# Four heads side by side on the array, and the other matmuls woven between them, in a gated mix of attention and FFN with its gradients

## The chip, the cores and the metric

The kernel runs on one core of one Trainium2 chip. The metric is device time in microseconds (us) of one execution. Unless a run says otherwise, times are medians of several executions.

## The reference, cut to what matters

The function computes a sigmoid gate `g`, a sliding-window attention `a` (32 heads of 16 features, window 256, sequence 2048, model width 512), a gated FFN `b` (width 1376), and the output `g * a + (1 - g) * b`. The kernel must return this output and the gradients of seven inputs.

```python
def _A_ref(x, wqkv, wo):
    H = 32; Dh = D // H; W = 256                    # Dh = 16
    q, k, v = ...                                   # (cut) x @ wqkv, split by head
    scores = jnp.einsum("bhqd,bhkd->bhqk", q, k) * (Dh ** -0.5)
    mask = (idx[:, None] - idx[None, :] >= 0) & (idx[:, None] - idx[None, :] < W)
    p = _softmax(jnp.where(mask[None, None], scores, -1e9), axis=-1)
    o = jnp.einsum("bhqk,bhkd->bhqd", p, v)
    return o.transpose(...).reshape(B, S, D) @ wo
def _B_ref(x, W_gate, W_up, W_down):
    gate = x @ W_gate; up = x @ W_up                # (written as einsum)
    return ((gate * (gate > 0)) * up) @ W_down
g = _sigmoid((x * gate_w).sum(-1, keepdims=True))
out = g * a + (1 - g) * b
def reference(..., grad_out):                       # (cut)
    _out, _vjp = jax.vjp(_f, A_x, A_wqkv, A_wo, B_W_gate, B_W_up, B_W_down, gate_w)
    return (_out, *_vjp(grad_out))
```

The backward pass of attention needs, for each head, the scores S, their exponentials P, the products dP = dO V^T, P * dP, and four weighted sums of these with K, V, Q and dO. The kernels compute them twice, once with queries and once with keys on the partitions.

## The kernel before: the parts that matter here

The program runs in stages: the FFN and its weight gradients, then attention in four groups of eight heads, then the weight gradients of the projections and the outputs. In attention, K and V are stored once for each head with zeros in the rows of the other seven heads (`KTz`, `VTz`), so that a matmul over all 128 rows gives the scores of one head. This is the pass by query blocks (the pass by key blocks is alike):

```python
for j in range(NT):                                  # 16 query blocks of 128
    kbs = list(range(max(0, j - 2), j + 1))
    ...
    for h8 in range(HG):                             # 8 heads
        ST = psA.tile([P, 3, P], F32, tag="ST")
        nc.tensor.matmul(ST[:, nb - 1, :], lhsT=ident[:], rhs=mbd[:, 0, :], ...)   # the mask
        for i, kb in enumerate(kbs):
            nc.tensor.matmul(ST[:, i, :], lhsT=KTz[:, h8, kb * P:(kb + 1) * P],
                             rhs=QT[:, j * P:(j + 1) * P], start=False, stop=True, ...)
        nc.scalar.activation(PuT[:, :nb, :], ST[:, :nb, :], ACT.Exp, scale=scale)
        ...                                          # affine_select on POOL where nb == 3
        for i, kb in enumerate(kbs):
            nc.tensor.matmul(dPT[:, i, :], lhsT=VTz[:, h8, kb * P:(kb + 1) * P],
                             rhs=dOT[:, j * P:(j + 1) * P], start=True, stop=True)
        nc.vector.tensor_tensor(out=PdPT[:, :nb, :], in0=PuT[:, :nb, :], in1=dPT[:, :nb, :], op=ALU.mult)
        for i, kb in enumerate(kbs):                 # 33 columns
            nc.tensor.matmul(Bacc[:, h8, :], lhsT=PuT[:, i, :], rhs=KV1[:, kb, h8, :], ...)
        for i, kb in enumerate(kbs):                 # 17 columns
            nc.tensor.matmul(Aacc[:, h8, :], lhsT=PdPT[:, i, :], rhs=KV1[:, kb, h8, 0:17], ...)
```

The softmax here doesn't subtract the row's maximum and nothing guards it: scores larger than these inputs give would overflow.

Of the kernel before, what the change touches and what calls it, by code (L numbers as in the profile page):

```python
# [9 lines left out]
ALU = mybir.AluOpType  # L10
# [3 lines left out]
I32 = mybir.dt.int32  # L14
# [4 lines left out]
WINDOW = 256  # L19


@with_exitstack
def kernel(
# [30 lines left out]
    assert Dh == 16 and D % P == 0 and S % P == 0 and WINDOW == 2 * P  # L54
    NT = S // P
    DC = D // P
    HG = P // Dh
    FC = (F + P - 1) // P
    TGW = min(512, S)
    NTG = S // TGW  # L60
    TPG = TGW // P
    scale = float(Dh) ** -0.5
    C3 = 3 * DC
# [3 lines left out]

    rr = {"i": 0}

    def evac(out, in_, eng=None):  # L70
        if eng is None:
            eng = ("act", "dve")[rr["i"] % 2]
            rr["i"] += 1
        if eng == "act":
            nc.scalar.copy(out, in_)  # L75
        elif eng == "dve":
            nc.vector.tensor_copy(out, in_)
        else:
            nc.gpsimd.tensor_copy(out, in_)

    def bc(ap2, n):
# [3 lines left out]
    hT_d = dram.tile([F, S], BF, name="hT_d")  # L85
    dgT_d = dram.tile([F, S], BF, name="dgT_d")
    duT_d = dram.tile([F, S], BF, name="duT_d")
    dqkv_d = dram.tile([S, 3 * D], BF, name="dqkv_d")
    O_d = dram.tile([S, D], BF, name="O_d")

    cpool = ctx.enter_context(tc.tile_pool(name="const", bufs=1))
    ident = cpool.tile([P, P], BF, name="ident")
    make_identity(nc, ident[:])
    NEG = -30000.0
    mbd = cpool.tile([P, 2, P], BF, name="mbd")
    nc.gpsimd.memset(mbd[:], 0.0)
    nc.gpsimd.affine_select(out=mbd[:, 0, :], in_=mbd[:, 0, :], compare_op=ALU.is_ge, fill=NEG,
                            base=0, pattern=[[1, P]], channel_multiplier=-1)
    nc.gpsimd.affine_select(out=mbd[:, 1, :], in_=mbd[:, 1, :], compare_op=ALU.is_ge, fill=NEG,
                            base=0, pattern=[[-1, P]], channel_multiplier=1)  # L100
    zeros_sb = cpool.tile([P, 512], F32, name="zeros_sb")
    nc.vector.memset(zeros_sb[:], 0.0)
    gw_b = cpool.tile([P, D], BF, name="gw_b")
    nc.sync.dma_start(gw_b[:], gate_w.partition_broadcast(P))
    g_all = cpool.tile([P, NT], F32, name="g_all")
    omg_all = cpool.tile([P, NT], F32, name="omg_all")
    z_all = cpool.tile([P, NT], F32, name="z_all")

    xT_pool = tc.tile_pool(name="xT", bufs=1, side="right")
    xT_pool_obj = xT_pool.__enter__()  # L110
    x_T = xT_pool_obj.tile([P, DC, S], BF, name="x_T")
    da_T = xT_pool_obj.tile([P, DC, S], BF, name="da_T")

    def transpose_rows_to_T(dst_T, src_r, psum_pool):
        for c in range(DC):
            for t0 in range(0, NT, 8):
                n = min(8, NT - t0)
                pt = psum_pool.tile([P, 8, P], BF, tag="tr")
                for k in range(n):
                    nc.tensor.transpose(pt[:, k, :], src_r[:, t0 + k, c * P:(c + 1) * P], ident[:])  # L120
                evac(dst_T[:, c, t0 * P:(t0 + n) * P].rearrange("p (k s) -> p k s", k=n), pt[:, :n, :])

    with ExitStack() as p12:
        actp = p12.enter_context(tc.tile_pool(name="acts", bufs=1))
        x_r = actp.tile([P, NT, D], BF, name="x_r")
        db_r = actp.tile([P, NT, D], BF, name="db_r")
        db_T = actp.tile([P, DC, S], BF, name="db_T")
        nc.sync.dma_start_transpose(out=x_T[:], in_=x_d)
        nc.sync.dma_start(x_r[:], x_d.rearrange("(t p) d -> p t d", p=P))

        ps2 = p12.enter_context(tc.tile_pool(name="p2ps", bufs=1, space=PSUM))

        def tr_rows(dst_T, src_r):
            for c in range(DC):
                for t0 in range(0, NT, 8):
                    n = min(8, NT - t0)
                    pt = ps2.tile([P, 8, P], BF, tag="tr", bufs=2)
                    for k in range(n):
                        nc.tensor.transpose(pt[:, k, :], src_r[:, t0 + k, c * P:(c + 1) * P], ident[:])
                    evac(dst_T[:, c, t0 * P:(t0 + n) * P].rearrange("p (k s) -> p k s", k=n), pt[:, :n, :])  # L140

        wp = p12.enter_context(tc.tile_pool(name="ffw", bufs=1))
        Wg_sb = wp.tile([P, DC, F], BF, name="Wg_sb")
        Wu_sb = wp.tile([P, DC, F], BF, name="Wu_sb")
        WdT_sb = wp.tile([P, DC, F], BF, name="WdT_sb")
        nc.scalar.dma_start(Wg_sb[:], B_W_gate.rearrange("(c p) f -> p c f", p=P))
        nc.scalar.dma_start(Wu_sb[:], B_W_up.rearrange("(c p) f -> p c f", p=P))
        fp = p12.enter_context(tc.tile_pool(name="ffn", bufs=2))
        with ExitStack() as p1:
            tmpp = p1.enter_context(tc.tile_pool(name="p1tmp", bufs=1))  # L150
            for c in range(DC):
                nc.scalar.dma_start_transpose(out=WdT_sb[:, c, :], in_=B_W_down[:, c * P:(c + 1) * P])
            gw_col = tmpp.tile([P, DC], BF, name="gw_col")
            nc.sync.dma_start(gw_col[:], gate_w.rearrange("(c p) -> p c", p=P))
            zps = ps2.tile([P, NT], F32, tag="wg", bufs=2)
            for t in range(NT):
                for c in range(DC):
                    nc.tensor.matmul(zps[:, t:t + 1], lhsT=x_T[:, c, t * P:(t + 1) * P], rhs=gw_col[:, c:c + 1],
                                     start=(c == 0), stop=(c == DC - 1))
            nc.scalar.activation(g_all[:], zps[:], ACT.Sigmoid)  # L160
            nc.vector.tensor_scalar(omg_all[:], g_all[:], -1.0, 1.0, op0=ALU.mult, op1=ALU.add)
            for t in range(NT):
                go_t = tmpp.tile([P, D], BF, tag="go_t", bufs=4)
                nc.gpsimd.dma_start(go_t[:], go_d[t * P:(t + 1) * P, :])
                nc.scalar.mul(db_r[:, t, :], go_t[:], omg_all[:, t:t + 1])
                da_t = tmpp.tile([P, D], BF, tag="da_t", bufs=3)
                nc.vector.tensor_scalar(da_t[:], go_t[:], g_all[:, t:t + 1], None, op0=ALU.mult)
                for src, dst in ((db_r[:, t, :], db_T), (da_t[:], da_T)):
                    pt = ps2.tile([P, 8, P], BF, tag="tr", bufs=2)
                    for c in range(DC):  # L170
                        nc.tensor.transpose(pt[:, c, :], src[:, c * P:(c + 1) * P], ident[:])
                    evac(dst[:, :, t * P:(t + 1) * P], pt[:, :DC, :])

        with ExitStack() as p2:
            for fc in range(FC):
                fs = fsz(fc)
                f0 = fc * P
                rg = fp.tile([P, S], BF, tag="rg")
                upm = fp.tile([P, S], BF, tag="upm")
                hT = fp.tile([P, S], BF, tag="hT")  # L180
                dgT = fp.tile([P, S], BF, tag="dgT", bufs=1)
                duT = fp.tile([P, S], BF, tag="duT", bufs=1)
                for tg in range(NTG):
                    ts_ = slice(tg * TGW, (tg + 1) * TGW)
                    gps = ps2.tile([P, TGW], F32, tag="mm", bufs=4)
                    ups = ps2.tile([P, TGW], F32, tag="mm", bufs=4)
                    for c in range(DC):
                        nc.tensor.matmul(gps[:fs, :], lhsT=Wg_sb[:, c, f0:f0 + fs], rhs=x_T[:, c, ts_],  # L188
                                         start=(c == 0), stop=(c == DC - 1))
                    for c in range(DC):  # L190
                        nc.tensor.matmul(ups[:fs, :], lhsT=Wu_sb[:, c, f0:f0 + fs], rhs=x_T[:, c, ts_],  # L191
                                         start=(c == 0), stop=(c == DC - 1))
                    nc.scalar.activation(rg[:fs, ts_], gps[:fs, :], ACT.Relu)
                    nc.vector.scalar_tensor_tensor(out=upm[:fs, ts_], in0=rg[:fs, ts_], scalar=0.0,  # L194
                                                   in1=ups[:fs, :], op0=ALU.is_gt, op1=ALU.mult)
                    nc.gpsimd.tensor_tensor(out=hT[:fs, ts_], in0=rg[:fs, ts_], in1=upm[:fs, ts_], op=ALU.mult)  # L196
                nc.sync.dma_start(hT_d[f0:f0 + fs, :], hT[:fs, :])
                for tg in range(NTG):
                    ts_ = slice(tg * TGW, (tg + 1) * TGW)
                    dhps = ps2.tile([P, TGW], F32, tag="mm", bufs=4)  # L200
# [222 lines left out]
    with ExitStack() as p56:  # L423
# [33 lines left out]
        with ExitStack() as p5:  # L457
# [12 lines left out]
            def load_round(ri, with_x=False):  # L470
                lo, hi = span(rounds[ri])
                if hi == lo:
                    return None, 0
# [199 lines left out]
```

## Time and profile before

| kernel before | |
|---|---|
| time | 1464.81 us, median of 3 runs (1462.81 to 1466.41) |
| feed-forward, from 0 us | about 330 us |
| attention, 330 to 1144 us | about 814 us |
| weight gradients and outputs, 1144 to 1465 us | about 321 us |
| matmuls | 16120 |

Some parts of the profile's page of the kernel before follow. Part 1 gives busy time and share of the span for each engine (PE is the matmul engine, PEld its weight loads, which overlap it). Part 2 cuts the span into 40 equal slices, each digit a busy share in tenths; PEclk is the granted clock of PE in tenths of full speed. Part 4 is the chain of work that ended last. Part 5 lists groups of instructions: line, engine, operation, out<-in, shapes, count, busy us, mean ns, then the idle time before them and what ended it.

```profile
...
PE 1226.8 (84%) x16120; PEld 882.4 (60%) x16120; DVE 805.4 (55%) x1801; ACT 733.6 (50%) x1706; POOL 677.2 (46%) x1894
...
PE   1899999996886998877988879988889558799996
...
PEclk9999999998998998998989989989979779899998
DMA  9212122123001011001030010110010692455530
...
PE 57%; ACT 12%; DVE 8%; POOL 7%; DMA 7%; issue 6%; ACTq 2%; SPq 1%; DVEq 0%; POOLq 0%
...
L331 DVE TENSOR_TENSOR PdPT<-PuT,dPT 128x384 bf16<-128x384 bf16 (+2 forms) x512 | 248.6, 521 | 66.1 <-POOL PuT L324 31.1
L322 ACT ACTIVATE PuT<-ST 128x384 bf16<-128x384 f32 (+2 forms) x512 | 230.6, 479 | 89.2 <-PE ST L318 68.2
...
L318 PE MATMUL ST<-QT,KTz 128*128 128x128 bf16 x1440 | 194.4, 224 | 1.9 <-DMA KTz<-KTn 1.8
...
L334 PE MATMUL BAp<-KV,PuT 128*128 128x33 bf16 x1440 | 117.0, 180 | 34.7 <-POOL PuT L324 31.6
...
```

The reader is to see two things. PE is busy in almost every slice, so PE is what bounds this kernel; the chain agrees with 57%. And PE's work is in small pieces: 1440 matmuls of 128 columns (224 ns each) for one of the four score products, whose 128 rows hold 16 that are not zero, and 1440 of 33 columns (180 ns each) for one of the four sums. The exp (ACT) and the product (DVE) are small as well, 128x384 at most.

The table of stretches shows the three stages; its columns are the stretch, its length, busy us of each engine with the number of instructions, the granted clock, the DMA share and GB/s.

```profile
...
core 0: us, PE busy (x) PEld busy (x) DVE busy (x) ACT busy (x) POOL busy (x), PEclk, DMA share, GB/s
0.00:330.00 330.00, 277.20 (x2128) 178.18 (x2128) 122.55 (x182) 115.65 (x183) 118.08 (x113) 0.98 0.30 97
330.00:1144.00 814.00, 686.96 (x12545) 576.90 (x12544) 603.78 (x1449) 568.76 (x1450) 505.11 (x1701) 0.94 0.08 19
1144.00:1465.00 321.00, 262.68 (x1448) 127.34 (x1448) 79.05 (x171) 49.22 (x73) 54.03 (x80) 0.91 0.52 161
...
```

In attention PE is busy 687 of 814 us, at a clock of 0.94, and the DMA engines hardly at all (0.08).

### The profile page before, as it was taken

The numbers are of one execution on the slowest core, as the hardware profiler recorded it, in microseconds if no ns is written. First come the engines' busy times: TensorE is split into PE (matmuls) and PEld (weight loads), VectorE is DVE, ScalarE is ACT, GpSimd is POOL, SyncE is SP. The second block draws the span as 40 slices with busy tenths as digits, with TensorE's granted clock in tenths as the row PEclk, the third lists the DMA queues.
The fourth block names the chain that finished last, engine by engine and source line by source line (L and its number), as shares of the span: only waits on it lengthen the run. The fifth ranks groups of instructions, "written<-read, shape, count | busy, mean of one in ns | idle before, by whom it ended". The sixth has DMA issues, their size and how long they took to land.

```text
span 1465.2 us, 40605 instructions
## 1 busy us (share of the span) xinstructions
PE 1226.8 (84%) x16120; PEld 882.4 (60%) x16120; DVE 805.4 (55%) x1801; ACT 733.6 (50%) x1706; POOL 677.2 (46%) x1894
## 2 busy tenths in 40 slices
PE   1899999996886998877988879988889558799996
PEld 0556556563776876767847768667778223444443
DVE  0534343434776975778947779757789202333332
ACT  0733232323775976766947759767669100311111
POOL 1434252434556863558825568635589203022111
PEclk9999999998998998998989989989979779899998
DMA  9212122123001011001030010110010692455530
GB/s 248 88 65 98 65 85 75 72 77 90 3 3 31 3 31 30 3 3 31 3 59 2 3 31 4 31 31 2 3 31 4 229 331 97 155 168 153 154 109 19
DMA packets 127249, 99.58 MB, mean 68 GB/s; under 512 B 65521, under 2 KB 112178, under 8 KB 127058
## 3 DMA queue, kind: packets, MB, share of 16 engines
q1 hardware_dynamic: 82034, 56.63, 12.6%
q10 hardware_dynamic: 40160, 27.76, 6.6%
q0 software_dynamic: 4864, 12.59, 2.9%
q8 instruction: 126, 2.06, 0.6%
q14 instruction: 65, 0.53, 0.1%
HBM read 52.92 MB, written 35.82 MB: 61 GB/s over the span
## 4 chain that ended last, share of the span: by engine, by line
PE 57%; ACT 12%; DVE 8%; POOL 7%; DMA 7%; issue 6%; ACTq 2%; SPq 1%; DVEq 0%; POOLq 0%
PE wps L227 5%; PE S L390 5%; ACT Pu L393 5%; PE dP L401 4%; ACT PuT L322 3%; POOL PuT L324 3%; PE dPT L328 3%; PE pp L276 3%; PE CDp L407 3%; PE dxps L624 3%; PE gps L188 3%; PE dps L234 3%; PE BAp L334 3%; DVE PdPT L331 3%; PE ups L191 3%
## 5 line engine op out<-in xcount | busy, mean ns | idle before, releaser
L331 DVE TENSOR_TENSOR PdPT<-PuT,dPT 128x384 bf16<-128x384 bf16 (+2 forms) x512 | 248.6, 521 | 66.1 <-POOL PuT L324 31.1
L322 ACT ACTIVATE PuT<-ST 128x384 bf16<-128x384 f32 (+2 forms) x512 | 230.6, 479 | 89.2 <-PE ST L318 68.2
L404 DVE TENSOR_TENSOR PdP<-Pu,dP 128x384 bf16<-128x384 bf16 (+2 forms) x512 | 246.2, 525 | 32.2 <-POOL Pu L397 16.4
L393 ACT ACTIVATE Pu<-S 128x384 bf16<-128x384 f32 (+2 forms) x512 | 228.7, 482 | 31.3 <-PE CDp L407 11.5
L390 PE MATMUL S<-KTz,QT 128*128 128x128 bf16 x1440 | 178.2, 225 | 32.1 <-DVE R L371 23.6
L324 POOL TENSOR_SCALAR_AFFINE_SELECT PuT<-PuT 128x128 bf16<-128x128 bf16 x448 | 131.8, 301 | 147.4 <-ACT PuT L322 147.1
L318 PE MATMUL ST<-QT,KTz 128*128 128x128 bf16 x1440 | 194.4, 224 | 1.9 <-DMA KTz<-KTn 1.8
L394 POOL TENSOR_SCALAR_AFFINE_SELECT Pu<-Pu 128x128 bf16<-128x128 bf16 x512 | 149.7, 295 | 46.1 <-ACT Pu L393 32.4
L401 PE MATMUL dP<-VTz,dOT 128*128 128x128 bf16 x1440 | 168.1, 222 | 0.0
L328 PE MATMUL dPT<-dOT,VTz 128*128 128x128 bf16 x1440 | 166.5, 221 | 1.3 <-DMA VTz<-VTn 1.2
L334 PE MATMUL BAp<-KV,PuT 128*128 128x33 bf16 x1440 | 117.0, 180 | 34.7 <-POOL PuT L324 31.6
L337 PE MATMUL BAp<-KV,PdPT 128*128 128x17 bf16 x1440 | 115.0, 173 | 33.4 <-DVE PdPT L331 32.0
L196 POOL TENSOR_TENSOR hT<-rg,upm 128x512 bf16<-128x512 bf16 (+1 forms) x44 | 50.7, 1154 | 194.3 <-DVE upm L194 194.3
L397 POOL TENSOR_SCALAR_AFFINE_SELECT Pu<-Pu 128x128 bf16<-128x128 bf16 x448 | 132.2, 295 | 0.0
L407 PE MATMUL CDp<-R,Pu 128*128 128x32 bf16 x1440 | 124.8, 178 | 3.6 <-POOL Pu L394 1.3
L390 PEld LDWEIGHTS <-QT 128*128 128x128 bf16 x1440 | 105.9, 100 | 30.3 <-DVE R L371 24.4
L318 PEld LDWEIGHTS <-KTz 128*128 128x128 bf16 x1440 | 115.5, 100 | 5.9 <-issue 2.9
L315 PE MATMUL ST<-mbd,ident 128*128 128x128 bf16 x512 | 113.7, 224 | 4.8 <-ACT KV L75 4.8
L337 PEld LDWEIGHTS <-PdPT 128*128 128x128 bf16 x1440 | 83.4, 98 | 52.6 <-DVE PdPT L331 48.6
L410 PE MATMUL CDp<-Qn,PdP 128*128 128x16 bf16 x1440 | 112.4, 171 | 0.6
L334 PEld LDWEIGHTS <-PuT 128*128 128x128 bf16 x1440 | 72.1, 96 | 55.3 <-POOL PuT L324 51.9
L410 PEld LDWEIGHTS <-PdP 128*128 128x128 bf16 x1440 | 88.2, 98 | 23.4 <-issue 13.1
(154 smaller groups left out, 2366.6 us busy)
## 6 DMA issues: line engine op xcount, KB each, us to landing
dqT_g<-dqkv_d SPq DMA_DIRECT2D x8, 768.0 KB, 16.1
hT_d<-hT SPq DMA_DIRECT2D x10, 512.0 KB, 2.6
dgT_d<-dgT SPq DMA_DIRECT2D x10, 512.0 KB, 3.1
duT_d<-duT SPq DMA_DIRECT2D x10, 512.0 KB, 2.9
hT_g<-hT_d SPq DMA_DIRECT2D x8, 640.0 KB, 5.5
dgT_g<-dgT_d ACTq DMA_DIRECT2D x8, 640.0 KB, 5.3
duT_g<-duT_d ACTq DMA_DIRECT2D x8, 640.0 KB, 6.3
go_t<-in_grad_out_dram POOLq DMA_DIRECT2D x32, 128.0 KB, 2.4
```

What stands on the lines that cost most here:

```text
L318: nc.tensor.matmul(ST[:, i, :], lhsT=KTz[:, h8, kb * P:(kb + 1) * P], rhs=QT[:, j * P:(j + 1) * P], start=False, stop=True, skip_group_che ...
L322: nc.scalar.activation(PuT[:, :nb, :], ST[:, :nb, :], ACT.Exp, scale=scale)
L324: nc.gpsimd.affine_select(out=PuT[:, 0, :], in_=PuT[:, 0, :], compare_op=ALU.is_ge, fill=0.0, base=-1, pattern=[[-1, P]], channel_multipli ...
L328: nc.tensor.matmul(dPT[:, i, :], lhsT=VTz[:, h8, kb * P:(kb + 1) * P], rhs=dOT[:, j * P:(j + 1) * P], start=True, stop=True)
L331: nc.vector.tensor_tensor(out=PdPT[:, :nb, :], in0=PuT[:, :nb, :], in1=dPT[:, :nb, :], op=ALU.mult)
L334: nc.tensor.matmul(Bacc[:, h8, :], lhsT=PuT[:, i, :], rhs=KV1[:, kb, h8, :], start=False, stop=True, skip_group_check=True)
L337: nc.tensor.matmul(Aacc[:, h8, :], lhsT=PdPT[:, i, :], rhs=KV1[:, kb, h8, 0:17], start=False, stop=True, skip_group_check=True)
L390: nc.tensor.matmul(S2[:, i, :], lhsT=QT[:, qb * P:(qb + 1) * P], rhs=KTz[:, h8, kb * P:(kb + 1) * P], start=True, stop=True)
L393: nc.scalar.activation(Pu2[:, :nb, :], S2[:, :nb, :], ACT.Exp, scale=scale)
L401: nc.tensor.matmul(dP2[:, i, :], lhsT=dOT[:, qb * P:(qb + 1) * P], rhs=VTz[:, h8, kb * P:(kb + 1) * P], start=True, stop=True)
L404: nc.vector.tensor_tensor(out=PdP2[:, :nb, :], in0=Pu2[:, :nb, :], in1=dP2[:, :nb, :], op=ALU.mult)
L410: nc.tensor.matmul(Dacc[:, h8, :], lhsT=PdP2[:, i, :], rhs=Qn[:, qb, h8, :], start=False, stop=True, skip_group_check=True)
```

## The change

The intent is to do the same arithmetic with fewer and fuller matmuls, and to leave PE no stage in which it waits for others. The change is nearly a new program. Its core:

- Scores: the four heads of a group lie on rows 0 to 31, 32 to 63, 64 to 95 and 96 to 127. A matmul uses 32 rows, and four such matmuls are meant to be in the array at once. K and V are no longer padded by head; only Q and dO keep zeros, in 16 of a head's 32 rows. The mask matmuls are gone.
- Sums: each head's sum goes to 32 columns of the array, four heads to one accumulator.
- One exp and one product cover two heads and 512 columns (before: one head, 384 columns).
- A "slot" is one such unit of two heads: PE makes the products dP of this unit and the scores S of the next but one, ACT the exp, DVE the product P * dP, POOL the mask. There are 384 units.
- Between the slots, `fill` places pieces of the FFN, the projections, weight gradients and dx ("steps", each about four matmuls of 512 columns), by a hand-made table of costs, so that what is left is spread evenly over the slots that are left.
- FFN rows and gradients are transposed by DMA, through DRAM, no longer on PE. All these loads, and most of the stores, are issued on one queue (that of SP).

```diff
-                            nc.tensor.matmul(ST[:, i, :], lhsT=KTz[:, h8, kb * P:(kb + 1) * P],
-                                             rhs=QT[:, j * P:(j + 1) * P], start=False, stop=True, ...
+            for i in (2 * u.r, 2 * u.r + 1):
+                rs = slice(32 * i, 32 * i + 32)
 ... (cut)
+                    lst.append(lambda ...: nc.tensor.matmul(
+                        bank[:, i % 2, col * P:(col + cnt) * P], lhsT=lt[rs, ls], rhs=rt[rs, rsl],
+                        start=True, stop=True))
 ... (cut)
+            u.dP = ps.tile([P, 2, W], F32, tag="dP", bufs=1, name="dP")
 ... (cut)
+            nc.vector.tensor_tensor(out=u.Pd[:, :, :u.width], in0=u.Pt[:, :, :u.width], in1=u.dP[:, :, :u.width],
+                                    op=ALU.mult)
 ... (cut)
+                    for i in range(4):
+                        wt = weights(a, i)
+                        nc.tensor.matmul(acc[32 * i:32 * i + wt.shape[1], q0:q0 + cnt * P], lhsT=wt,
+                                         rhs=m[:, i % 2, col * P:(col + cnt) * P], ...)
 ... (cut; in the step that makes the FFN gradient)
+                    nc.vector.tensor_tensor(out=q["dgT"][:fs, :], in0=dhs[:fs, :], in1=q["upm"][:fs, :], op=ALU.mult)
+                    nc.gpsimd.tensor_tensor(out=q["duT"][:fs, :], in0=dhs[:fs, :], in1=q["rg"][:fs, :], op=ALU.mult)
+                    for w, nm in enumerate(("hT", "dgT", "duT")):
+                        nc.sync.dma_start(ffn_d[fc, w, :fs, sl], q[nm][:fs, :])
 ... (cut)
+                        nc.sync.dma_start_transpose(out=rw[:]..., in_=ffn_d[fc, :, :, sl]...)
 ... (cut)
+        def fill(slot, used, later, nxt_dve, nxt_pool):
+            share = todo["pe"] / max(1, todo["slot"])
 ... (cut)
+            while used["pe"] < share:
 ... (cut: take the first step whose engines are free in this slot)
```

After the last slot a short stage remains, called the tail: the weight gradient of one group of heads, the gradient of `wo`, and the outputs in 16 tiles.

## The prediction

> **What bounds the kernel now.** The busy shares give PE 84%, DVE 55%, ACT 50%, POOL 46%; the chain that ended last is 57% PE, ACT 12%, DVE 8%, POOL 7%, DMA 7%. The stretch table gives three stages: feed-forward (0 to 330 us), attention (330 to 1144 us, 56% of the span), and weight gradients plus output (1144 to 1465 us). In attention PE is busy about 86%, DVE, ACT and POOL 60 to 80%. The groups show why: 5,760 score matmuls 128x128 whose contraction holds only 16 live rows of 128 (K and V zero-padded per head), 5,760 small products (128x16 to 128x33), and 512 mask matmuls. A head and query block needs 13 matmuls; at about 0.78 us that is 60 ns each.
>
> **What the change does.** Four heads share the array: scores use 32 rows per head, the weighted sums 32 columns per head. One exp and one product now cover 2 heads x 512 columns. FFN, projections and most of dx are woven between 386 attention slots; most transposes go from PE to DMA through DRAM. The compiled order has about 9,750 matmuls (before 16,120), DVE 597 instructions (before 1,801), POOL 725, ACT 678, but over 900 DMAs on the SP queue.
>
> **Costs of the woven stretch, from durations in the trace.**
> - PE, full array: 1.107 M columns. A 512-column matmul repeats every 0.216 us in the chain: 467 us.
> - PE, scores: 737 k columns in four row groups. The Trainium skill, "TensorE: Matmul & The Clock Gate", Part 3, measured 3.07x for four row groups; no run here shows it yet. Estimate 100 to 155 us.
> - PE, weighted sums: 912 k columns in four column groups, estimate 125 to 165 us.
> - 875 changes of tiling mode, each a drain (the skill, "TensorEngine Tiling (Array Packing)", Key Properties; untested here): guess 50 to 90 us.
> - DVE: the product at 128, 256, 384 columns takes 287, 413, 548 ns, so 1,024 should take 1.22 us; with the rest 600 to 640 us. ACT: exp 277, 396, 501 ns, so 1.05 us; about 560 us. POOL: 736 wider selects, estimate 0.45 to 0.85 us each, plus products of 1.15 to 1.3 us; 620 to 660 us.
> So PE still sets the pace: about 810 us, 2.1 us a slot; with a clock near 0.96 and small waits, 835 to 870 us. Before the slots about 50 us (loads, transposes, first projections), after them about 85 us (PE about 60).
>
> Off the critical path: padded score work, mask matmuls, the serial FFN stage (about 280 us; its matmuls remain), boundary waits (1150 to 1200: PE 29 of 50 us).
>
> **Predicted time 980 us, 80% range 890 to 1100.** Chances: faster 0.97, same 0.01, slower 0.02.
>
> **What would show it.** Right: attention slots of about 2.1 to 2.2 us; PE the largest share of the chain; DVE, ACT and POOL each 60 to 75% busy; product near 1.22 us, exp near 1.05 us; clock at 0.95 or better. Wrong: slots above 2.5 us, or PE waiting on loads or POOL.
>
> **What would make it wrong.** Row groups not overlapping (scores 300 us; about 1,150 total). The SP queue: the 2 MB transpose held it 18.7 us (estimate 9 us per MB; some 40 MB now) and plain issues cost 0.34 to 0.39 us, so 500 to 650 us; if it falls behind, 1,100 or more. Better packing and free mode changes: 880.

## The result, and the profile after

| | before | after |
|---|---|---|
| time, median | 1465.37 us, 15 runs (1462.79 to 1468.38) | 1080.06 us, 12 runs (1073.82 to 1092.0) |
| ratio to before | | 0.7363, 95% interval 0.7344 to 0.7383 |

Here and below a ratio is the mean time of one kernel's fast runs over the mean time of the other's fast runs of the same rounds, so it is not quite the ratio of the medians quoted, which count slow runs too. The change won 26%. It lies inside the predicted range of 890 to 1100 us, but 100 us above the predicted 980 us. Executions over 1.5% slower than the fastest of the same kernel are left out of the means. Two of the 12 runs, at 1090.4 and 1092.0 us, counted as slow; the profiled execution, 1087.5 us, was fast.

The page of the changed kernel, the same parts as before:

```profile
...
PE 884.9 (81%) x9748; PEld 424.7 (39%) x9748; DVE 675.7 (62%) x797; ACT 578.5 (53%) x842; POOL 595.4 (55%) x983
...
PE   5876898998889889997769679999999877534785
...
PEclk9999899999999999999879889999999999666999
DMA  7456656656556676554368977668675521286174
...
L512 DVE TENSOR_TENSOR Pd<-Pt,dP 128x1024 bf16<-128x1024 bf16 (+2 forms) x384 | 442.9, 1153 | 292.2 <-PE S L475 146.1
...
L508 ACT ACTIVATE Pt<-S 128x1024 bf16<-128x1024 f32 (+2 forms) x384 | 372.4, 970 | 199.3 <-PE S L475 174.6
L475 PE MATMUL dP<-kv,dO 32*128 32x384 bf16 (+2 forms) x704 | 75.3, 283 | 33.1 <-DVE Pd L512 32.7
...
```

PE works 885 us, not 1227. The product takes 1153 ns on average (1220 ns at full width) and the exp 970 ns (1023 ns at full width). The clock row shows 9 nearly everywhere, but 8 near 120 us, 7 to 9 from 515 to 650 us, and three slices of 6 near the end. The DMA engines, idle in the attention of before, are now at half load throughout. The chain of the page cannot be used here: it broke off at the last instructions, with shares of 0%, so what follows rests on stretches, waits and the timeline.

One slot, from the timeline near 302 us (columns: start us, length us, engine, line, operation, out<-in, shapes, count, and the idle time before it with its releaser):

```profile
...
301.00 0.83 PE L525 MATMUL acc<-Pd,R 128*16 128x384 bf16 x24
...
301.21 1.02 ACT L508 ACTIVATE Pt<-S 128x1024 bf16<-128x1024 f32 x1 [1.05 <-PE S L475]
301.27 1.22 DVE L512 TENSOR_TENSOR Pd<-Pt,dP 128x1024 bf16<-128x1024 bf16 x1 [0.26 <-PE S L475]
...
301.76 1.04 PE L224 MATMUL mm<-db_T,woT 128*128 128x512 bf16 x4
...
302.73 0.28 PE L475 MATMUL dP<-dO,kv 32*128 32x256 bf16 x2
302.74 0.39 PE L475 MATMUL S<-Q,kv 32*128 32x128 bf16 x4
...
303.06 1.04 PE L347 MATMUL mm<-db_r,rows 128*128 128x512 bf16 x4
...
```

The reader is to see the packing at work: 24 matmuls of the sums, 6144 columns, are done in 0.77 us (until the next matmul starts at 301.76, the end being modelled), and the eight score matmuls, 2048 columns in all, take 0.33 us (302.73 to 303.06). In between stands one FFN step of four matmuls, 0.97 us from start to the next start. Where no tiling change follows, the same step takes 0.86 to 0.88 us; so a change away from the full array costs about 0.1 us (e1 tests this too).

By starts of the product, the median slot took 2.15 us, as predicted (2.1 to 2.2). But the mean was 2.34 us: 44 slots took over 3 us and hold 90 us above 2.1 us. The stretches after, with the columns of the table before:

```profile
...
565.00:665.00 100.00, 76.53 (x939) 44.11 (x939) 50.90 (x49) 49.10 (x83) 42.96 (x79) 0.87 0.85 184
665.00:765.00 100.00, 99.39 (x1122) 42.69 (x1121) 64.97 (x64) 59.53 (x81) 56.35 (x104) 1.00 0.68 185
915.00:965.00 50.00, 22.13 (x318) 11.61 (x311) 22.35 (x25) 16.59 (x24) 16.31 (x31) 0.67 0.49 127
...
```

From 665 to 765 us PE is full (99.39 of 100). From 565 to 665 us it is not (76.53), while the DMA share is at its highest, 0.85; and at 915 to 965 us, where the slots end and the tail begins, it is busy 22 of 50 us and the clock is down to 0.67. PE's waits (waiter <- releaser: us in total, times, longest us):

```profile
...
PE dP L475 <- DVE Pd L512: 55.6, 69, 5.8
PE dw L757 <- DMA R<-DKV_d: 17.7, 1, 17.7
PE mm L757 <- DMA R<-DKV_d: 15.8, 2, 9.1
...
PE dxps L975 <- DMA lt<-DQO_d: 8.7, 2, 5.3
...
```

These are: the products dP waiting for the DVE product to free their single PSUM buffer (55.6 us in 69 short waits); loads of the gradient rows R, stalls of 9.1 us and 6.8 us in the slots and 17.7 us at the start of the tail; and loads in the tail (lt, 8.7 us). Adding up PE's gaps in the trace between 35 and 945 us gives 126 us idle: 24 until 165 us, 29 until 465 us, 23 until 565 us, 23 until 665 us, 6 until 865 us and 22 in the last 80 us. The prediction had allowed 25 to 60 us for clock and waits together. The tail, from the last product at 943.6 us to the end at 1085.8 us, took 142 us; the prediction said 85.

### The profile page after: what moved, and what is told of

Same layout as the page of the kernel before. It is cut to its first block, busy times and chain, and to the rows that moved or that the text cites. A ratio compares the mean times of both kernels' runs of the same rounds, so it can differ in the third digit from the quotient of the medians.

```text
span 1085.8 us, 25091 instructions
## 1 busy us (share of the span) xinstructions
PE 884.9 (81%) x9748; PEld 424.7 (39%) x9748; DVE 675.7 (62%) x797; ACT 578.5 (53%) x842; POOL 595.4 (55%) x983
## 5 line engine op out<-in xcount | busy, mean ns | idle before, releaser
L512 DVE TENSOR_TENSOR Pd<-Pt,dP 128x1024 bf16<-128x1024 bf16 (+2 forms) x384 | 442.9, 1153 | 292.2 <-PE S L475 146.1
L485 POOL TENSOR_SCALAR_AFFINE_SELECT Pt<-Pt 128x256 bf16<-128x256 bf16 (+1 forms) x736 | 343.2, 488 | 343.5 <-ACT Pt L508 337.4
L508 ACT ACTIVATE Pt<-S 128x1024 bf16<-128x1024 f32 (+2 forms) x384 | 372.4, 970 | 199.3 <-PE S L475 174.6
L475 PE MATMUL dP<-kv,dO 32*128 32x384 bf16 (+2 forms) x704 | 75.3, 283 | 33.1 <-DVE Pd L512 32.7
L334 PE MATMUL mm<-rows,x_r 128*128 128x256 bf16 (+1 forms) x704 | 87.2, 273 | 10.2 <-DMA rows<-ffn_d 7.5
L475 PE MATMUL dP<-dO,kv 32*128 32x128 bf16 (+2 forms) x704 | 73.9, 280 | 23.1 <-DVE Pd L512 23.0
L334 PEld LDWEIGHTS <-x_r 128*128 128x128 bf16 x704 | 64.9, 98 | 30.2 <-issue 20.4
L475 PE MATMUL S<-kv,Q 32*128 32x384 bf16 (+2 forms) x704 | 74.9, 284 | 0.2 <-ACT Pt L508 0.2
L757 PE MATMUL mm<-R,x_r 128*128 128x256 bf16 x448 | 60.8, 288 | 17.0 <-DMA R<-DKV_d 15.8
L475 PE MATMUL S<-Q,kv 32*128 32x128 bf16 (+2 forms) x704 | 73.7, 279 | 0.0
L757 PEld LDWEIGHTS <-x_r 128*128 128x128 bf16 x512 | 50.2, 103 | 52.1 <-DMA R<-DKV_d 27.7
L733 PE MATMUL mm<-WgT,grp 128*128 128x512 bf16 (+1 forms) x176 | 68.1, 387 | 0.0
L298 POOL TENSOR_TENSOR duT<-dhs,rg 128x512 bf16<-128x512 bf16 (+1 forms) x44 | 54.5, 1238 | 0.0
```

The lines of the kernel that those rows point to most:

```text
L298: nc.gpsimd.tensor_tensor(out=q["duT"][:fs, :], in0=dhs[:fs, :], in1=q["rg"][:fs, :], op=ALU.mult)
L334: nc.tensor.matmul(v["b"][:, 0:2 * fs], lhsT=x_r[:, t, c * P:(c + 1) * P], rhs=rows[t // 4][:, t % 4, 1:3, :fs], start=(t == 0), stop=(t = ...
L475: lst.append(lambda lt=lt, ls=ls, rt=rt, rsl=rsl, i=i, rs=rs, col=col, cnt=cnt: nc.tensor.matmul(bank[:, i % 2, col * P:(col + cnt) * P], ...
L485: nc.gpsimd.affine_select(out=v.rearrange("p h (b k) -> p h b k", b=cnt), in_=v.rearrange("p h (b k) -> p h b k", b=cnt), compare_op=ALU.i ...
L508: nc.scalar.activation(u.Pt[:, :, :u.width], u.S[:, :, :u.width], ACT.Exp)
L512: nc.vector.tensor_tensor(out=u.Pd[:, :, :u.width], in0=u.Pt[:, :, :u.width], in1=u.dP[:, :, :u.width], op=ALU.mult)
```

## The experiments

Three questions were open. Is it the packing or the weaving that brought the gain? Where do the missing 100 us sit, and why? Can they be had? My first theory for the last two was order on the one SP queue: cheap stores and urgent loads stand behind transposing loads of 1.2 to 2.4 us each. The rivals were the transfers themselves, the hand-made table, and the engines DVE and POOL.

### e1_full_scores: the scores over all 128 rows

```diff
-                rs = slice(32 * i, 32 * i + 32)
+                rs = slice(0, P)
```

Each head now gets the sum over the four heads of its group, which is wrong.

> The changed kernel, but each score matmul contracts over all 128 rows instead of its head's 32 (same matmuls, same columns, same waits; the result is wrong on purpose: each head gets the sum of four heads). Theory A, that four row groups running at once is a large part of the gain: the block of 8 score matmuls of a slot, now 0.33 us, should take about 0.87 us (2,048 columns at 2.4 per ns), two mode changes per slot go (estimate 0.1 us back), so 384 slots grow by about 0.45 us: 1,260 us, 1,220 to 1,300. Rival B, that the changed kernel is paced by the other engines and by transfers and the packing only made room nobody needs: 1,080 to 1,110 us. In this run's trace, a full-array block of 4 matmuls ahead of the scores, now 0.97 us, should fall to 0.87 us if the 0.1 us is the price of the mode change.

Measured: 1192.49 us (1189.45 to 1195.53, 2 runs), ratio 0.8156 (0.81 to 0.8212). These inputs are small, and the comparison is weak on the scores, so it does not vouch for this part. In the timeline a block of scores took 0.87 us against 0.33 where a step over the full array followed, and 0.97 us where the sums followed:

```profile
...
301.07 0.49 PE L475 MATMUL dP<-kv,dO 128*128 128x384 bf16 x2
...
302.04 0.67 PE L525 MATMUL acc<-Pt,ones 128*32 128x384 bf16 x16
...
```

From 301.07 to 302.04 is 0.97 us: a change to the tiling of the sums stands behind this block. The third expectation held as well: the four full-array matmuls ahead of the scores, 0.96 to 0.97 us in the changed kernel, took 0.86 us here, so the 0.1 us is the price of the change of tiling. The total rose by 112 us and not by 180, which is below the expected range of 1220 to 1300: the median slot grew by 0.41 us only, probably since part of the added work went into time in which PE had been waiting. So the row packing, undone alone, is worth about 110 us of the result.

### e2_full_sums: the sums over all 128 columns

```diff
-        ones32 = mc.tile([P, 32], BF, name="ones32")
+        ones32 = mc.tile([P, P], BF, name="ones32")
...
-                        nc.tensor.matmul(acc[32 * i:32 * i + wt.shape[1], q0:q0 + cnt * P], lhsT=wt,
+                        nc.tensor.matmul(acc[:, q0:q0 + cnt * P], lhsT=wt,
...
-                return st["kvr", n + d][:, k, 32 * i:32 * i + 32]
+                return st["kvr", n + d][:, k, :]
```

> The changed kernel, but each weighted-sum matmul uses 128 columns of the array instead of its head's 32 (same number of matmuls and streamed columns; wrong on purpose). Theory A: a sweep of 24 matmuls, 6,144 columns, now 0.77 to 0.84 us, should take 2.6 us; about 148 full sweeps' worth of columns, so plus 255 us: 1,335 us, 1,290 to 1,370. Rival B: 1,080 to 1,110 us.

Measured: wrong (relative error 1.98); 1289.17 us (1281 to 1297, 2 runs), ratio 0.8817 (0.8685 to 0.895).

```profile
...
400.21 2.79 PE L525 MATMUL acc<-Pt,kvr 128*128 128x384 bf16 x24
...
402.84 1.03 PE L267 MATMUL mm<-x_T,wg 128*128 128x512 bf16 x4
...
```

The 24 matmuls took 2.63 us (400.21 to 402.84), against 0.77 us. The column packing is worth about 209 us. In both experiments the expected direction and mechanism held; both totals came out below the expected ranges, which came from plain adding, probably because PE had idle time to fill.

### e3_unwoven: packing without weaving

```diff
+            if slot < nslots:
+                return out                       # only projections may be placed between slots
...
-            while used["pe"] < share:
+            while used["pe"] < share and (projs or slot >= nslots):
```

FFN, weight gradients and dx then run after the last slot, with the same steps in the same code.

> The changed kernel, but feed-forward, most of dx and the weight gradients run after the last attention slot instead of between the slots (the three later projections stay between them). Theory A2, that weaving is worth about as much as the packing because the attention slots alone are held at about 1.8 us by the chain scores, product, scores through one buffer of dP: 384 slots at 1.8 us, about 700 us, with the matrix engine less than half busy, then about 450 us of dense matmuls, then the same end: 1,345 us, 1,290 to 1,400. Rival B2, that only the amount of matrix work counts: the slots alone would run at about 0.7 to 1.25 us (matrix engine 0.33 us, product 1.22 us, overlapped), and the total stays below 1,150 us.

Measured: correct; 1481.74 us (1481.09 to 1482.38, 2 runs), ratio 1.0134 (1.0101 to 1.0168). The whole gain is gone, more than either theory had. The page tells why:

```profile
...
PE 1031.9 (70%) x9697; PEld 515.6 (35%) x9748; DVE 676.4 (46%) x797; ACT 593.0 (40%) x842; POOL 598.0 (40%) x983
...
PE   6765566556575655555565575888896668999875
...
PEclk9965577655585666555566787999998879999999
...
```

From the 4th to the 22nd slice PE is mostly busy 50 to 70%, and the granted clock is mostly 5 to 7 tenths; in the stretch 100 to 300 us it averaged 0.66, in 700 to 800 us 0.57. A block of scores took 0.55 us, against 0.33 us in the woven kernel, and the sums 1.40 us where no wait is counted in, against 0.77 us. The slots were hardly shorter for having less work: 2.02 us in the median, and PE waited 272.5 us, in 249 waits, for the product to free the one dP buffer. I had costed PE's work at the woven kernel's clock. The longest idle time of PE between 100 and 800 us was 1.46 us. So weaving does two things here: it fills the time PE would wait in, and with it the clock was 0.96 on average over the slots (0.87 to 1.00 in stretches of 100 us, 0.79 in the last 30 us). Of e3 both runs agree within 0.1%, and its clock was back at 0.97 from 1200 us on, while in the slow trace of `after_again` below it was 0.62 to 0.70 in every stretch, also where PE was 94% busy.

The 400 us are an upper figure for weaving. After the last slot the same steps took 524 us (817 to 1341 us), and PE was idle for 105 of these, 43 us of them for the transposed FFN rows: the order and margins were made for the weave, and a stage written for itself could probably avoid some of that. e1 to e3 ran on another chip than the later runs; by the ratios to the kernel before instead of the medians, the losses of e1, e2 and e3 are 116, 213 and 405 us.

### after_again, e5_stores, e6_margin, e7_tail: four runs on one chip

`after_again` is the changed kernel, unaltered, as a control.

> The changed kernel once more, unaltered, on the same chip as the three kernels sent with it, so that differences of one or two per cent can be read against it. Expected: 1080 us (1074 to 1090), ratio to the kernel before 0.736 plus or minus 0.003.

Measured: 1088.0 us median of 4 runs, ratio 0.7386 (0.736 to 0.7411). Two of its four runs were slow (1093.79 us, and the profiled one, 1283.39 us at a clock of 0.648); the two fast ones took 1082.21 and 1077.11 us.

`e5_stores` moves stores off the SP queue:

```diff
-                    nc.sync.dma_start(dst_d[c][sb]..., cs[:])
+                    eng_ = nc.sync if which == 3 else nc.scalar
+                    eng_.dma_start(dst_d[c][sb]..., cs[:])
...
-                        nc.sync.dma_start(ffn_d[fc, w, :fs, sl], q[nm][:fs, :])
+                        nc.gpsimd.dma_start(ffn_d[fc, w, :fs, sl], q[nm][:fs, :])
```

> Stores taken off the one in-order load queue: the projections' K, V and Q stores go to the scalar engine's queue, the FFN rows' stores to the POOL queue; every byte stays. Theory (a cheap store waits behind a transposing load of 1.2 to 2.4 us on the same queue, and its staging buffer then holds up ACT and PE): the stalls that the trace of the changed kernel shows near 85, 104 to 111 and 510 to 517 us go, with the waits on the store of the row buffers (7.3 us in POOL, 7.3 in DVE, 6.5 plus 4.1 in ACT): 15 to 25 us less, so 1055 to 1065 us, 20 us off the run of the unaltered kernel beside it. Rival (the queue's order doesn't matter; the transfers themselves, at a DMA share of 0.57, are late, or another wait takes the place): less than 6 us of difference, 1074 to 1086 us.

Measured: correct; 1137.01 us (1129.95 to 1143.43, 4 runs), ratio 0.7762 (0.7726 to 0.7798): 55 us slower than the control beside it. The theory failed. The named waits on the stores did leave the lists (the 7.3 us of POOL's hT and the 7.3 us of DVE's dgT are gone), but something else grew:

```profile
...
PE 893.3 (78%) x9638; PEld 433.4 (38%) x9748; DVE 709.1 (62%) x797; ACT 579.5 (51%) x842; POOL 661.1 (58%) x1115
...
L298 DVE TENSOR_TENSOR dgT<-dhs,upm 128x512 bf16<-128x512 bf16 (+1 forms) x44 | 74.4, 1692 | 1.6
...
```

POOL is busy 661 us, 66 us more, since it now issues 132 stores of about 0.55 us each. And DVE's product dgT, which nobody touched, takes 1692 ns on average; in the changed kernel it took 906 ns. The timeline of e5 shows one of them:

```profile
...
115.67 3.10 DVE L298 TENSOR_TENSOR dgT<-dhs,upm 128x512 bf16<-128x512 bf16 x1
...
116.22 1.16 POOL L286 TENSOR_TENSOR hT<-rg,upm 128x512 bf16<-128x512 bf16 x1
...
117.34 1.15 POOL L299 TENSOR_TENSOR duT<-dhs,rg 128x512 bf16<-128x512 bf16 x1
...
```

dgT starts at 115.67 us and ends at 118.77 us, 0.28 us after POOL's duT has ended (118.49). POOL had done masks, hT and duT back to back. In the changed kernel the same holds: of its 44 dgT all overlap POOL; the shortest take 0.41 us, and a dgT that meets a whole hT takes 1.43 us, ending 0.28 us after it:

```profile
...
140.45 1.15 POOL L285 TENSOR_TENSOR hT<-rg,upm 128x512 bf16<-128x512 bf16 x1 [1.59 <-DVE upm L283]
140.46 1.43 DVE L297 TENSOR_TENSOR dgT<-dhs,upm 128x512 bf16<-128x512 bf16 x1
...
```

The Trainium skill, "SBUF — State Buffer", section "Who interferes with whom", says that a DVE instruction with two SBUF inputs contends with a GpSimd (POOL) instruction that reads SBUF, and that the ports which the two share are an exclusive lock. The traces agree, with these numbers: 0.41 to 0.42 us with no POOL operation beside it (seen in e9 and e11), 1.43 us behind one whole POOL product. Here the later one waited: where dgT started 0.05 us before hT, dgT took its 0.42 us, and hT 1.39 us instead of 1.15. DVE's P * dP, which reads one operand from PSUM, kept 1.22 us whether POOL worked or not. So in e5 a busier POOL held DVE longer, DVE's product came later, and PE waited for it (81.0 us on dP against 55.6). A second path shows in the waits: POOL's own masks came later, and DVE's product waited 84.9 us for them, against 46.5. How much each path cost was not separated. The loss lies where the moved stores are: the first 200 products, the FFN half of the weave, took 546 us against 502 in the changed kernel, the other 184 some 393 us in both.

`e6_margin` gives the R loads more time:

```diff
-                    ready_at["dw"] = v2["at"][rq[0][0]] + 9
+                    ready_at["dw"] = v2["at"][rq[0][0]] + 14
```

> One constant: a weight-gradient step may be placed 14 slots after its transposing load was issued, not 9. Theory (the hand table's margin is too short: two stalls of 9.1 and 6.8 us near 600 us come from a matmul that heads PE's in-order queue before its load has landed, and nothing else could pass it): these two stalls go and most of their time with them, 10 to 16 us less, 1064 to 1070 us. Rival (PE's work has to wait anyway: with the steps later the fill runs short elsewhere, in the last 80 us above all): the stalls go from the list, but the time stays within 5 us of the unaltered kernel beside it.

Measured: correct; 1089.07 us (1084.46 to 1104.4, 4 runs, of which the slowest counted as slow), ratio 0.744 (0.7411 to 0.7468): not faster than the control. The two stalls on that load in the slots are gone from PE's waits, and two others stand in their place: 12.2 us for the V rows of attention and 7.3 us for the first dx group. The theory failed and the rival was nearer, though by the ratios the time was some 8 us above the control (the intervals just touch), not within 5, and the stalls shifted in the queue and not to the end of the weave.

`e7_tail` changes only the tail:

```diff
-        for w in range(3):                       # moved behind the loads needed first
-            nc.sync.dma_start_transpose(out=wl[:, w], in_=A_wqkv[:, ...])
...
-            pt = ps5.tile([P, 8, P], BF, tag="tr", bufs=1)
+            pt = ps5.tile([P, 8, P], BF, tag="dxps", bufs=3, name="pt5")
...
-            nc.scalar.activation(jk[:], pj[:], ACT.Copy, accum_out=dz[:, 0:1])
-            nc.vector.tensor_tensor(out=dz[:, 1:2], in0=g_all[:, t:t + 1], in1=omg_all[:, t:t + 1], op=ALU.mult)
-            nc.vector.tensor_tensor(out=dz[:, 2:3], in0=dz[:, 0:1], in1=dz[:, 1:2], op=ALU.mult)
+            nc.scalar.activation(jk[:], pj[:], ACT.Identity, scale=gomg[:, t:t + 1], accum_out=dz[:, 0:1])
... (stores on SP, dxps with 3 buffers, the end of a tile issued one tile later: cut)
```

> Only the stage after the weave, 141 us in the changed kernel against 85 predicted. Three edits: the late weight gradient's transposing load is issued first, ahead of three weight loads that are needed last (PE was idle 17.7 us for it, 9.8 us of that the loads ahead); the transposes of the output gradient stage get three PSUM buffers, not one (its loop took 1.9 us a tile against some 1.2 us of PE work); in the output loop two small DVE operations that took 0.90 us a tile go (the product of gate factors is made once, and scaling rides on the accumulating copy), stores leave POOL's queue, and the closing operations of a tile are issued one tile later (3.37 us a tile against 2.83 us of DVE work left). Theory (order and single buffers make the length of this stage): 8 to 10 plus 8 to 11 plus 7 to 9 us less, so a stage of about 113 to 118 us and 1053 to 1058 us in all. Rival (the half clock near 965 us and the transfers set the pace): less than 12 us gained in all, 1068 us or more.

Measured: correct; 1057.76 us (1053.58 to 1062.4, 4 runs), ratio 0.7237 (0.7212 to 0.7262). The tail took 112.5 us (948.2 to 1060.7), against 142.2 us. So the theory held in sum, but not in its parts. The time from the last product to the first output tile fell from 82.0 to 54.5 us, more than the 16 to 21 us expected; the output loop itself fell only from 3.37 to 3.11 us a tile in the median, not to 2.83, and with a slower start (one tile took 8 us) the whole loop fell by 2 us only. The three edits were not run apart. The groups of the changed kernel show what the loop had paid:

```profile
...
L988 DVE TENSOR_TENSOR dz<-dz 128x1 f32<-128x1 f32 x16 | 12.3, 766 | 0.6 <-ACT jk L986 0.6
L979 DVE SCALAR_TENSOR_TENSOR o_sb<-amb,g_all,b_t 128x512 bf16<-128x512 f32 x16 | 11.8, 740 | 0.0
...
```

An operation on one element for each partition took 766 ns; its neighbour of the same kind (L987) took 146 ns. It stood behind POOL's pj, and ended when that ended. In e7 this operation is gone, and another with two SBUF operands met pj instead:

```profile
...
L982 DVE SCALAR_TENSOR_TENSOR o_sb<-amb,g_all,b_t 128x512 bf16<-128x512 f32 x16 | 20.0, 1252 | 0.0
...
```

o_sb went from 740 to 1252 ns. The wait had changed its owner.

### e8_kvact, e9_dut, e10_pace: three edits on top of e7

These three ran on another chip than e7, so they are set against e7 by their ratios to the kernel before, which ran beside each of them.

`e8_kvact` keeps the first half of e5's diff (K, V and Q stores on ACT's queue) and leaves POOL alone.

> The tail edits of e7 plus one half of e5: the projections' K, V and scaled Q stores go to the scalar engine's queue, the FFN rows' stores stay where they were. The run of e5 lost 55 us although the waits for these stores left its list. Theory (e5 lost because POOL then made 132 stores of 0.55 us itself, 73 us, and DVE's product of two SBUF operands stood still while POOL worked, 1692 ns against 906 ns): without POOL's part that loss is gone, dgT is at 0.9 us again, POOL's busy time is that of e7, and what is left is the gain from not waiting behind transposing loads: 4 to 12 us below e7, so 1046 to 1054 us, ratio 0.715 to 0.721. Rival (the scalar engine's stores themselves cost e5 its time, or no order of the queue matters): 1055 us or more.

Measured: correct; 1060.08 us (1055.53 to 1064.47, 4 runs), ratio 0.7241 (0.7216 to 0.7267), the same as e7. dgT was at 919 ns and POOL at 580 us, so e5's loss did come from giving these stores to POOL, as the theory said. But its other half failed: the order of these stores on the queue was worth nothing that could be measured. Of the rival's two halves, the one that the order doesn't matter stands.

`e9_dut` changes one word:

```diff
-                    nc.gpsimd.tensor_tensor(out=q["duT"][:fs, :], in0=dhs[:fs, :], in1=q["rg"][:fs, :], op=ALU.mult)
+                    nc.vector.tensor_tensor(out=q["duT"][:fs, :], in0=dhs[:fs, :], in1=q["rg"][:fs, :], op=ALU.mult)
```

> The tail edits of e7 plus one word: the FFN product duT runs on DVE, not POOL. In the changed kernel DVE's dgT and POOL's duT start together, and dgT, whose mean is 906 ns, ends when POOL's operation ends; the shortest full-width ones take about 0.42 us. Theory (while POOL works on SBUF, a DVE operation with two SBUF operands waits): dgT falls to 0.4 to 0.6 us, duT takes 0.4 to 0.6 us on DVE against 1.24 on POOL, DVE's busy time rises by less than 10 us though it does 44 more products, and the time falls by 2 to 10 us below e7: 1047 to 1056 us, ratio 0.716 to 0.723. Rival (906 ns is what dgT costs): dgT stays near 0.9 us, DVE's busy time rises by some 40 us, and the time is 1058 us or more.

Measured: correct; 1053.02 us (1051.2 to 1054.62, 4 runs), ratio 0.7183 (0.7163 to 0.7202), some 8 us below e7 by the ratios (5 us by the medians). Its four runs also lie below all runs of e8 and all but one of e10 (1054.39 us) on the same chip.

```profile
...
L298 DVE TENSOR_TENSOR duT<-dhs,rg 128x512 bf16<-128x512 bf16 (+1 forms) x44 | 38.0, 863 | 0.0
...
L297 DVE TENSOR_TENSOR dgT<-dhs,upm 128x512 bf16<-128x512 bf16 (+1 forms) x44 | 34.1, 774 | 1.7
...
```

The time was right, the sizes were not: dgT took 774 ns and duT 863 ns, not 400 to 600, and DVE's busy time rose by 28 us, not under 10. The instances show why. The four duT with no POOL operation beside them took 0.41 us, the others waited for masks or other products of POOL (mean 0.91 us). And the traces do not show where the gain lies: the first 200 products, the part of the weave that holds every duT, took 504 us here, 507 in e7 and 501 in e8, and POOL makes duT in both of these. So the gain is shown by the times alone; that it comes from DVE standing still less is not shown.

`e10_pace` thins out the loads at the hand-over from the FFN half to the second half of the weave:

```diff
-            if v2.get("loads"):
+            if v2.get("loads") and slot % 2 == 0:
...
-                ready_at["dw"], ready_at["bx"] = slot + 9, slot + 24
+                ready_at["dw"], ready_at["bx"] = slot + 14, slot + 44
```

> The tail edits of e7 plus a slower hand-over between the two halves of the weave: the 18 loads of the second half's weights, most of them transposing, are issued one every second slot, not every slot; the dx steps may start 44 slots after the hand-over, not 24; weight-gradient steps 14 slots after their load, not 9. In e6 the margin alone moved the stalls from the weight-gradient load to other loads on the same queue (12.2 us on the V rows of the attention, 7.3 us on the first dx group). Theory (the queue is oversubscribed near 570 to 630 us, and which load is late only depends on the order): with half the rate all these stalls shrink, from 16 to 27 us to under 6 us, and the work pushed back fills the last 80 us of the weave, where PE was idle 21 us: 8 to 16 us below e7, 1041 to 1050 us, ratio 0.712 to 0.718. Rival (PE's work is only moved, and the end of the weave then overflows into the tail): 1055 us or more.

Measured: correct; 1058.09 us (1054.39 to 1062.56, 4 runs), ratio 0.7219 (0.7193 to 0.7246), not to be told from e7. The R stalls left the list, and one stall of 14.9 us on the V rows came. SP's part of the timeline shows what was before them:

```profile
...
643.48 0.37 SPq L576 DMA_DIRECT2D UV_d<-V  x1
...
645.92 2.34 SPq L578 DMA_TRANSPOSE R<-UV_d  x1
...
```

V had been computed on DVE at 612.5 to 613.2 us. Its store to DRAM (L576) was issued at 643.48 us, 30 us later, and the transposing load of it (L578) at 645.92 us; PE went on at 651 us. From 590 to 650 us the queue issued one transfer after another (56 of 60 us). So it is oversubscribed there, and pacing only chose another victim.

### e11_dve and e12_plain

`e11_dve` also moves hT to DVE (`late_pool` then holds a `nc.vector.tensor_tensor`), on top of e9's edit.

> The tail edits of e7, and both FFN products that POOL made, hT and duT, on DVE. In e9 a dgT that started with no POOL operation in progress took 0.42 us, one that started inside POOL's hT took until that ended plus 0.28 us, up to 1.43 us; so its mean fell only to 774 ns. Theory (POOL's operations of 1.2 us are what DVE's two-operand products wait for): without hT on POOL, dgT falls to 0.45 to 0.65 us and duT to 0.5 to 0.75 us, POOL's busy time falls from 539 to some 486 us, DVE's rises from 699 to 700 to 715 us, and the time falls below e9's ratio of 0.718: 0.711 to 0.717, some 1042 to 1050 us. Rival (DVE is by now the engine that the FFN half of the weave waits for, so that work added to it costs as much as the waits saved): 0.717 or more.

Measured: correct; 1055.18 us (1052.9 to 1056.7, 4 runs), ratio 0.7202 (0.7185 to 0.7219), not below e9. That is what the rival expected.

```profile
...
L297 DVE TENSOR_TENSOR dgT<-dhs,upm 128x512 bf16<-128x512 bf16 (+1 forms) x44 | 26.6, 604 | 0.0
...
L298 DVE TENSOR_TENSOR duT<-dhs,rg 128x512 bf16<-128x512 bf16 (+1 forms) x44 | 22.6, 513 | 0.0
...
```

The mechanism did what it should (604 and 513 ns, hT 560 ns, each 0.41 us where POOL is silent; POOL's busy time 485 us). But the three products now share one engine in order: ACT's copy of dh waited 12.3 us for DVE's duT, against 7.7 in e9, and PE behind it.

`e12_plain` replaces ten transposing loads of the second half's weights by plain loads of the same bytes; dx has wrong numbers.

```diff
-                    L.append(lambda a=a, w_d=w_d, wT=wT: nc.sync.dma_start_transpose(
-                        out=wT[:, a:a + 2, :], in_=w_d[:, a * P:(a + 2) * P]))
+                    L.append(lambda a=a, w_d=w_d, wT=wT: nc.sync.dma_start(
+                        wT[:, a:a + 2, :].rearrange("p a (k f) -> p (a k) f", f=2 * P),
+                        w_d[:, a * P:(a + 2) * P].rearrange("(k p) f -> p k f", p=P)))
```

> The tail edits of e7, with the ten transposing loads of the second half's gate and up weights replaced by plain loads of the same bytes: the dx output is wrong on purpose, everything else is as in e7. It asks whether the stalls near 600 us come from these loads' way of transferring. Theory (transposing loads fill the one in-order queue: ten of 1.3 us and more at 577 to 600 us, so that what is behind them is late): PE's idle time in 565 to 665 us falls from 26.9 to 8 to 14 us, the stall of the weight-gradient load (15.2 us in two) to under 6, and the time is 8 to 16 us below e7, ratio 0.713 to 0.718. Rival (the weight-gradient loads are transposing loads of half a megabyte themselves, or the attention's stores they read land late; the weights don't matter): the stalls keep at least 12 us, the ratio is 0.721 or more.

Measured: 1047.72 us (1039.82 to 1050.11, 4 runs), ratio 0.7135 (0.7102 to 0.7168), about 15 us below e7 by the ratios (10 us by the medians). PE's idle time from 565 to 665 us fell from 26.9 to 19.0 us (expected 8 to 14), and the wait for R to half:

```profile
...
PE mm L758 <- DMA R<-DKV_d: 7.3, 2, 4.6
...
```

In e7 this line read 15.2 us, longest 9.1. SP spent 16 us on transposing loads between 565 and 615 us, not 32. In the profiled runs 9 of the 12 us gained lie between products 200 and 240, which took 96 us, not 105; the stretches before and after changed by about 1 us or less. So half of the wait for R, and 8 of the 27 us that PE is idle near the hand-over, are due to these loads' transposing; the rest, and the 56 us of waits for the product, no run took away.

The fastest kernel with correct results is e9_dut, at 1053.02 us, 2.4% below the changed kernel by the ratios (0.7183 to 0.7363); e11_dve can't be told from it.

## Why the prediction was right, and where it was wrong

- **The direction and most of the size: right.** The packing is worth about 112 us (e1) and 209 us (e2) when each part is undone alone; the weaving about 400 us (e3). The last is an upper figure. They do not add up, probably since each uses idle time that the others leave. The wider exp and product, the dropped mask matmuls and the transposes by DMA came with the change and were not undone alone, so their shares stay open. That weaving also holds up the clock was not in the prediction, which said "with a clock near 0.96" as if it were given; it was 0.96 in the slots, but e3 at 0.57 to 0.70 shows that it has to be earned.
- **Costs of single operations: right.** Product 1.22 us predicted and measured; exp 1.05 predicted, 1.02 measured; the scores, 0.33 us for 2048 columns, about 119 us for 737 thousand columns, in the predicted 100 to 155; the sums, 0.77 us for 6144 columns, about 115 us for 912 thousand columns, just under the predicted 125 to 165. PE's busy time from 35 to 945 us, 910 less 126 us, is 784 us; predicted were 810. With 467 us for the full array, what is left for the 875 changes of tiling and the clock below full speed is about 85 us (an estimate from these figures); guessed were 50 to 90 for the changes alone.
- **The median slot: right** (2.15 us, against "about 2.1 to 2.2 us").
- **"With a clock near 0.96 and small waits, 835 to 870 us": wrong, and the main step that failed.** The slots took 895 us (48.4 to 943.6). PE waited 126 us, where the prediction left 25 to 60 us for clock and waits together; the clock was as said, so the waits are the term that was too small. The parts found: the hand-over of loads near 600 us, 23 us, of which some 8 us are shown by e12 to be the transposing weight loads; 5 to 8 us that e9 won by moving one product from POOL to DVE, its path not shown; waits for the product through one dP buffer, 56 us over the whole run, 21 of them in the last 80 us when the steps had run out, which is read in the trace and was not tested. The rest was not taken apart.
- **"After them about 85 us (PE about 60)": wrong by 57 us.** The tail took 142 us, with PE busy 79 us of it. Its work was costed, too low, and its waits were not. e7 shows that some 30 us were order, single buffers and small DVE operations together, 27 of them before the output loop. Of the rest, 14 us is the load of R, and in the output loop of 3.1 us a tile DVE is busy nearly all the time.
- **"The SP queue ... 500 to 650 us; if it falls behind, 1,100 or more": the size was right, the consequence half right.** It was busy about 630 us between 35 and 945 us. It fell behind in places only: near 600 us (e10, e12), not where I looked first (e5, e8). PE waiting on loads was one of the prediction's own signs of being wrong, and there it was seen (15.8 us for R in the slots).
- **"DVE, ACT and POOL each 60 to 75% busy": a little high** (62, 53 and 55%), as the span was longer. "PE the largest share of the chain" could not be judged, as the chain broke off.

In sum: predicted 50 + 852 (the middle of the range) + 85 is 987 us; measured in the profiled run 48 + 895 + 142 is 1086 us. Of the 99 us, 43 are the slots (126 us of waits, in part made up for by PE's work, 26 us less than predicted) and 57 the tail. The result lies inside the range, near its upper end, because the range was wide enough for these waits; it named the loads as a risk but had not costed them.

## What to carry to other kernels

When work is woven so that one engine is full on paper, cost the waits as a term of their own: a mean slot is its median plus the slots that stall, and they stall where many loads change hands at once, and at the ends. Moving an operation to a less busy engine is not free even if that engine has time: look first at what its instructions hold up, as POOL's did DVE's here. And when a wait vanishes from the list and the time stays, look for the line in which it has come back.

## What the Trainium skill lacked or had wrong

- "SBUF — State Buffer", section "Who interferes with whom", has the rule that fits the DVE times of e5, e9 and the tail, and two ratios, but no times for such products: here a 128x512 bf16 product on DVE took 0.42 us alone and 1.43 us behind one POOL product of 1.15 us, up to 3.3 us behind several (e5), and an operation of one element for each partition 766 ns, not 146.
- "TensorE: Matmul & The Clock Gate", Part 1, gives as its rule that PE should have no idle times of over about 3.4 us. That was not enough here: in e3 no idle time of PE between 100 and 800 us was longer than 1.46 us, and the mean granted clock was 0.57 to 0.66. The section on queue cycling names short idle times as a cause, without a number.
- The same page, Part 3, has 3.07 times for four row groups and 2.38 times for three column groups. Here four row groups did 2048 columns in 0.33 us, against 0.87 us over the full array in e1 (2.6 times), and four column groups 24 matmuls in 0.77 us against 2.63 us in e2 (3.4 times).
- "TensorEngine Tiling (Array Packing)", Key Properties, says that changing the mode drains the array, without a price: about 0.1 us for a change away from the full array here (0.96 to 0.97 against 0.86 to 0.88 us for four matmuls).
- "DMA: Bandwidth & Descriptors" gives DMA transposes a bandwidth (261 GB/s) and, for small tiles, a decode time in cycles, but not how long a large one holds its queue: here 1.2 to 3.9 us for each of the woven loads and 18.7 us for one of 2 MB in the kernel before, during which nothing else on that queue was issued.
